# The first phase of a Fourier mixing and squared-ReLU kernel: four mirrored joins moved to the second block, small tables put on GpSimd's queue, another order

## The chip, the cores and the metric

The kernel runs on one NeuronCore of one Trainium2 chip. The metric is the device time of one execution in microseconds (us), as the median of several runs. A core has TensorE (PE in the profile; matrix products into PSUM), VectorE (DVE), ScalarE (ACT), GpSimd (POOL) and SyncE (SP, which issues most DMAs here). Each engine works through its own instructions in the order in which the program lists them and waits on semaphores for the others.

## The reference

All data are float32, with 8 sequences of 3008 rows and 256 columns.

```python
X = np.fft.fft(x, axis=1)            # x: (8, 3008, 256)
X = np.fft.fft(X, axis=2)
y = X.real.reshape(8 * 3008, 256)
h = y @ w_in                         # (256, 2048)
r = np.maximum(h, 0.0)
out = (r * r) @ w_out                # (2048, 256)
```

The real part of the double transform is a cosine transform along both axes less a sine transform along both axes.

## The kernel before, in words

**Folds.** The symmetry of sines and cosines is used before any product. Each sequence comes as seven tiles of rows (`TILES`, classes 0 to 3: one tile of class 0, one of class 1, two of class 2, three odd ones). `fold(0, t)` has six pieces. `for_p(t)` does three: a sum (line L485), the sum of mirrored columns (L501) and two combinations (L515), with a small ScalarE copy (L518) for the middle column E. `for_q(t)` does the other three: a difference (L489), L505 and two more L515. The results lie in tiles `w`, of which there are eight buffers.

**Transforms along the rows.** The products (L632) of the `w` tiles with tables of cosines and sines, `cosT` and `sinT`, collect in PSUM, for P (cosine) and Q (sine), each for even and odd columns (`kp` 0 and 1). The middle column E rides along as the last row of Q. A short radix chain joins them on VectorE: `join_4` and `join_2` put the even classes together, then `join_1` combines this with the odd part, its lower half into columns 0 to 752 of `Pt` or `Qt` (`lo`: L674 for P, L669 for Q), its mirrored upper half into columns 753 to 1504 (`hi`: L678 and L671). P's joins read PSUM and SBUF; so do Q's, which also apply signs.

**Weights.** The transform along the 256 columns is folded into `w_in`: `begin_win(j)` splits the raw 64-bit numbers of one of eight pairs of column blocks (L274, L276), ScalarE makes powers of two (L280, L281), `rounded(j)` puts halves and product together (L291, L293, L300), and TensorE multiplies with the column tables `cosd` and `sind` (L315); ScalarE copies the results to `G1` and `G2` (L316). With `shared`, a conversion on ScalarE (L283) and a product on GpSimd (L298) stand in for L300. `gE` (L324, L326) is the factor for E.

**Steps.** Then 384 steps follow: 8 sequences, 6 blocks of 251 columns each, 8 pairs `j`. `front` makes four products (L838, L839) into PSUM tiles of tag `h` (two buffers), and VectorE adds E's share and forms the sum and the difference (L841, L843, L844). `combine` squares on ScalarE (L853, L854), and from the second block on GpSimd makes four sums (L861 to L864). `back`, two steps later, multiplies with `w_out` (L878, L891). In steps 0 to 7 the remaining weights are converted; in steps 8 to 11 VectorE forms sums of `w_out` (L341 to L345). From step 10 the next sequence's folds and joins are woven into the steps.

**E.** Each front reads row E spread over all partitions (`Et`). `spread_e` makes its first 251 columns by a product (L816) and a copy (L817); `spread_rest` stores the row to DRAM and loads the other 1254 columns, both on GpSimd's queue (L821, L822).

**Order.** The scheduler is off (`manual_schedule`): the first phase is written out by hand, and each engine's and each queue's order is that of the code. Before step 0 SP issues, in this order, x tiles 0 and 1, raw win 0, x 2 and 3, `cosd`, `sind` and its last column `alt_d`, the table parts of classes 0 and 1 (six issues), x 4 and 5, those of class 2 (four), x 6, the wide tables of the odd class, raw win 1, ten small issues of `sinT`, raw win 2. `awake(n)` gives TensorE n products that fill time and that nobody reads. In steps 8 on, SP is busy with `load_column` (L408), single columns of the next sequences, and the outputs.

Of the kernel before, what the change touches and what calls it, by code (L numbers as in the profile page):

```python
# [13 lines left out]
P = 128  # L14
# [68 lines left out]
def kernel(  # L83
# [108 lines left out]
    G2 = const.tile([P, F], F32, name="G2")  # L192
    gE = const.tile([P, NFC], F32, name="gE")

    def load_table(tab, src, tiles):

        for t in tiles:
            c, r0, step, rows = TILES[t]
            for i, (s0, count) in enumerate(row_tiles(S)):
                mine = [r for r in range(count) if (s0 + r - r0) % step == 0 and 0 <= (s0 + r - r0) // step < rows]  # L200
                if mine:
                    o, m = (s0 + mine[0] - r0) // step, len(mine)
                    while m % 15 and m % 16 and o + m < P and mine[0] + step * m < P:
                        m += 1
                    nk = NC[0][c]
                    nc.sync.dma_start(out=tab[o:o + m, :, PLACE[t]:PLACE[t] + nk],
                                     in_=src[mine[0]:mine[0] + step * (m - 1) + 1:step, :, i, 0:nk])

    make_identity(nc, ident)
    last = ident[:, P - 1:]  # L210
# [394 lines left out]
    def dft_ops(b):  # L605
# [7 lines left out]
        def group(kp, which):  # L613
# [6 lines left out]
            def product(ps, c, lone_e=False, only=None):  # L620

                ts = [t for t in range(NT) if TILES[t][0] == c]
                for t in ts if only is None else ts[only:only + 1]:
                    rows = TILES[t][3]
                    if b is None:
                        w = we[0:rows, SPOT[t], kp]
                    elif lone_e:
                        w = lone[0:rows, 2 * t + kp]
                    else:
                        w = folded[b, t][0:rows, kp, PART[which]]  # L630
                        w = w if which else w[:, 0:n]
# [16 lines left out]
            def copy_4():  # L648
                a = st["a"] = hp.tile([P, 2 * P], F32, name="da", tag="da", bufs=2)[0:n]
                nc.scalar.copy(a[:, 0:n2], st["ps"][0:n, 0:n2])  # L650

            def even_part(c, lone_e):

                if c == 0 and lone_e == both_in:
                    pool, tag = (psm, ("mC", "mD")[kp]) if both_in else (psd, "d")
                    st["ps"] = pool.tile([P, 512], F32, name="pd", tag=tag)
                at, nk = EVEN[c][1:]
                product(st["ps"][:, at:at + nk], c, lone_e)
                if c == 2 and not lone_e:
                    copy_4()  # L660

            def both(lo, hi, a, ps, only=None):

                nk, nh = a.shape[-1], hi.shape[-1]
                if both_in:

                    join = nc.vector.scalar_tensor_tensor
                    if only != 1:
                        join(out=lo, in0=ps, scalar=signs[:, 0:1], in1=a, op0=ALU.mult, op1=ALU.add)  # L669
                    if only != 0:  # L670
                        join(out=hi[:, ::-1], in0=a[:, 0:nh], scalar=signs[:, 1:2], in1=ps[:, 0:nh],  # L671
                             op0=ALU.mult, op1=ALU.add)
                    return
                tt(out=lo, in0=a, in1=ps, op=ALU.add)  # L674
                if which == 1:
                    tt(out=hi[:, ::-1], in0=ps[:, 0:nh], in1=a[:, 0:nh], op=ALU.subtract)
                else:
                    tt(out=hi[:, ::-1], in0=a[:, 0:nh], in1=ps[:, 0:nh], op=ALU.subtract)  # L678

            def join_4():  # L680
                a, ps = st["a"], st["ps"]
# [2 lines left out]

            def join_2():
                a, ps = st["b"], st["ps"]
                st["c"] = hp.tile([P, NC[0][3]], F32, name="dc2", tag="dc2", bufs=2)[0:n, 0:n0]
                both(st["c"][:, 0:n1], st["c"][:, n1:n0], a, st["half"] if b != 0 else ps[:, 2 * n2:2 * n2 + n1])

            def odd_part(i, lone_e):  # L690
# [93 lines left out]
                     st["odd"], only)  # L784

            if b == 0:
                named = [("join_4", join_4), ("join_2", join_2), ("lo", join_lo), ("hi", join_hi),
                         ("join_1", join_1)]
                for i in range(3):
                    for nm, f in (("even", even_part), ("odd", odd_part)):  # L790
                        named += [(nm + ("", "_e")[e] + str(i), lambda i=i, e=e, f=f: f(i, e == 1)) for e in range(2)]
                return [((which, kp, nm), f) for nm, f in named]
            ops = [(0.0, even_n), (0.5, join_4), (0.7, join_2), (0.0, odd_n), (1.1, join_1)]
            from_psum.update((join_4, join_2, join_turned))
# [21 lines left out]
        nc.tensor.matmul(ps, last.to_broadcast([P, P]), qt[:, 0:CK], start=True, stop=True)  # L816
        nc.scalar.copy(et[:, 0:CK], ps)  # L817

    def spread_rest():
        _, qt, et = PQE[0]  # L820
        nc.gpsimd.dma_start(out=e_dram[0:1], in_=qt[P - 1:P])  # L821
        nc.gpsimd.dma_start(out=et[:, CK:], in_=e_dram[0:1, CK:].to_broadcast([P, NKT - CK]))  # L822

    def load_e(b):
        nc.sync.dma_start(out=PQE[b][2], in_=e_dram[b:b + 1].to_broadcast([P, NKT]))
# [205 lines left out]
        product()  # L1031


    start()
    awake(48)
    for t in range(2):
        load_x(0, t)
    for_p(0)
    for_q(0)
    for_p(1)  # L1040
    begin_win(0)
    load_x(0, 2)
    load_x(0, 3)
    for dst, src in ((cosd, cos_d), (sind[:, :, 0:P - 1], sin_d), (sind[:, :, P - 1:], alt_d)):
        nc.sync.dma_start(out=dst, in_=src.rearrange("(c p) m -> p c m", p=P))
    load_table(cosT, cos_s, (0, 1))
    load_x(0, 4)
    load_x(0, 5)
    load_table(cosT, cos_s, (2, 3))
    load_x(0, 6)  # L1050
    load_table(cosT, cos_s, range(ODD0, NT))
    load_table(sinT, sin_s, range(ODD0, NT))
    win[1] = load(pair_in(1))
    load_table(sinT, sin_s, range(ODD0))
    win[2] = load(pair_in(2))
    for_p(2)
    rounded(0)
    win[0][1]()
    awake(2)
    for_p(3)  # L1060
    p_part("even0", "even1")
    q_part("even_e0", "even_e1")
    awake(6)
    p_part("even2")
    q_part("even_e2")
    for_q(1)
    for_p(4)
    for_p(5)
    for_q(2)
    for_p(6)  # L1070
    p_part("odd0", "odd1", "odd2")
    q_part("odd_e0", "odd_e1", "odd_e2")
    groups[0, 0, "join_4"]()
    groups[0, 0, "join_2"]()
    for_q(4)
    groups[0, 1, "join_4"]()
    groups[0, 1, "join_2"]()
    for_q(5)
    p_part("join_1")
    for_q(6)  # L1080
    q_part("odd0", "odd1", "odd2")
    copy_e = win[0][2]()
    begin_win(1)
    for_q(3)
    q_part("even0", "even1", "even2")
    awake(12)
    rounded(1)
    for kp in range(2):
        for nm in ("join_4", "join_2", "lo"):
            groups[1, kp, nm]()  # L1090
        if kp == 0:
            begin_win(2)
    spread_e()
    q_part("hi")
    copy_e()
    spread_rest()
# [78 lines left out]
    for i in range(len(steps) + LAG + 4):  # L1175
        if i < len(steps):
            b, k0, n, j = steps[i]
            if i == NJ:
                for k in range(NX):
                    load_later(k)  # L1180
            if NJ <= i < NJ + NL:
                load_column(i - NJ)
            if i % per == 0:
                assert not side
                side = ahead(b + 1) if b + 1 < B else []
                spent, pace = 0.0, sum(t for t, _ in side) / sum(share(i + k) for k in range(per - 2))
            multiply()
            g = front(b, k0, n, j, between)
            if i < NJ:
                weights()  # L1190
                s = combine(n, g, True)
            elif i < 2 * NJ:
                if j < 4:
                    sum_wout(slice(j // 2 * (NJ // 2), (j // 2 + 1) * (NJ // 2)), j % 2)
        while finished and finished[0][0] <= i:
            store(*finished.pop(0)[1:])
        if i >= LAG and flight:
            at, g_, s_ = flight.pop(0)
# [75 lines left out]
```

## Time and profile before

| | |
|---|---|
| median of 4 runs | 1922.74 us (1919.18 to 1923.81) |
| the profiled execution | 1919.18 us, its span 1917.4 us |
| busy: PE, PEld (weight loads) | 1907.4 us (99%), 1699.2 us (89%) |
| busy: DVE, ACT, POOL | 1444.9 us (75%), 953.3 us (50%), 1120.9 us (58%) |
| DMA | 69.58 MB; 225, 240 and 260 GB/s in the first three stretches of 10 us |
| first product of step 0 | at 40.85 us |

The span runs from the first to the last instruction; the time of the execution has 1.8 us more around it. A busy share is an average over the whole span. Times in the text are from the span's start. A line of a timeline gives start, duration, engine, line, operation, written and read tiles with their sizes, and, in brackets, an idle time before it with what ended it. In the slices of the page a digit is the busy share in tenths.

### The profile page before, as it was taken

To read this page: it belongs to the slowest core of one execution; us is meant where nothing else is said; L and a number is where in the kernel's file an instruction comes from. 1 tells how busy PE (TensorE), PEld (TensorE's weight loads), DVE (VectorE), ACT (ScalarE), POOL (GpSimd) and SP (SyncE) were. 2 spreads that over 40 slices of the span, in tenths; PEclk is the share of its full clock that TensorE was granted. 3 is DMA by queue.
4 is the path that set the end of the run, shared out by engine and by line. 5 is a ranking of instruction groups with operands and counts; after the bars stand their busy time and mean duration, and the time that the engine had idled before them with its cause. 6 is when DMAs were issued, how large, how long until landed. Compare 5 with 4: busy or idle time off the path is not lost.

```text
span 1917.4 us, 28162 instructions
## 1 busy us (share of the span) xinstructions
PE 1907.4 (99%) x9270; PEld 1699.2 (89%) x9270; DVE 1444.9 (75%) x3646; ACT 953.3 (50%) x1201; POOL 1120.9 (58%) x1709
## 2 busy tenths in 40 slices
PE   9999999999999999999999999999999999999998
PEld 8888898888988898888988889888898888988887
DVE  8988887787678876788768877788767777655554
ACT  2755554555454544455544454455544555444444
POOL 0265655665566665665566665566655665566565
PEclk9999999999999999999999999999999999999999
DMA  7331201110011101111011100111001101000100
GB/s 227 116 38 28 56 28 36 28 45 13 28 36 42 34 12 36 32 43 28 12 36 47 36 20 12 47 39 34 22 20 44 36 12 22 28 12 12 22 11 23
DMA packets 146622, 69.58 MB, mean 36 GB/s; under 512 B 130145, under 2 KB 137259, under 8 KB 146474
## 3 DMA queue, kind: packets, MB, share of 16 engines
q1 hardware_dynamic: 146022, 66.87, 13.8%
q8 instruction: 73, 1.20, 0.3%
q14 instruction: 75, 0.61, 0.1%
q0 software_dynamic: 176, 0.65, 0.1%
q10 hardware_dynamic: 276, 0.26, 0.0%
HBM read 43.03 MB, written 24.69 MB: 35 GB/s over the span
## 4 chain that ended last, share of the span: by engine, by line
PE 95%; DVE 3%; DMA 0%; ACT 0%; issue 0%; POOL 0%; DVEq 0%; ACTq 0%
PE ph L838 17%; PE ph L839 17%; PE mC L891 16%; PE mA L891 16%; PE mB L891 16%; PE mD L891 8%; PE pd L740 1%; PE mA L878 1%; PE mB L878 1%; PE pd L714 1%; PE pd L632 1%; DVE w L515 0%; DMA xt<-in_x_dram 0%; PE pg L315 0%; DVE fs L485 0%
## 5 line engine op out<-in xcount | busy, mean ns | idle before, releaser
L853 ACT ACTIVATE g<-g 128x1004 f32<-128x1004 f32 (+1 forms) x384 | 399.3, 1040 | 691.4 <-DVE g L844 445.9
L841 DVE SCALAR_TENSOR_TENSOR he<-Et,gE,ph 128x251 f32<-128x251 f32 (+1 forms) x768 | 362.5, 472 | 342.9 <-PE ph L839 338.5
L861 POOL TENSOR_TENSOR s<-g 128x251 f32<-128x251 f32 (+1 forms) x376 | 236.6, 629 | 636.8 <-ACT g L854 576.4
L838 PE MATMUL ph<-Pt,G 128*128 128x251 f32 (+1 forms) x1536 | 452.5, 375 | 0.4 <-DVE g L844 0.3
L839 PE MATMUL ph<-Qt,G 127*128 127x251 f32 (+1 forms) x1536 | 451.3, 374 | 0.0
L854 ACT ACTIVATE g<-g 128x1004 f32<-128x1004 f32 (+1 forms) x384 | 399.6, 1041 | 12.2
L891 PE MATMUL mC<-s,wsum 128*128 128x251 f32 (+1 forms) x1504 | 381.4, 374 | 0.0
L891 PE MATMUL mA<-g,wout 128*128 128x251 f32 (+1 forms) x1504 | 380.1, 374 | 0.0
L843 DVE TENSOR_TENSOR g<-he,ph 128x251 f32<-128x251 f32 (+1 forms) x768 | 320.4, 417 | 53.5 <-POOL s L861 1.4
L839 PEld LDWEIGHTS ph<-Qt,G 127*128 127x128 f32 x1536 | 291.3, 190 | 35.7
L838 PEld LDWEIGHTS ph<-Pt,G 128*128 128x128 f32 x1536 | 285.5, 189 | 34.6 <-DVE g L844 0.8
L891 PEld LDWEIGHTS mC<-s,wsum 128*128 128x128 f32 x1504 | 285.5, 190 | 34.5
L844 DVE TENSOR_TENSOR g<-he,ph 128x251 f32<-128x251 f32 (+1 forms) x768 | 314.0, 409 | 0.0
L891 PEld LDWEIGHTS mA<-g,wout 128*128 128x128 f32 x1504 | 282.6, 189 | 35.2 <-issue 0.3
L862 POOL TENSOR_TENSOR s<-s,g 128x251 f32<-128x251 f32 (+1 forms) x376 | 270.6, 720 | 29.5
L863 POOL TENSOR_TENSOR s<-g 128x251 f32<-128x251 f32 (+1 forms) x376 | 272.3, 724 | 0.0
L864 POOL TENSOR_TENSOR s<-g,s 128x251 f32<-128x251 f32 (+1 forms) x376 | 241.7, 643 | 0.0
L891 PE MATMUL mB<-g,wsum 128*128 128x251 f32 (+1 forms) x752 | 220.4, 374 | 0.0
L891 PE MATMUL mD<-s,wout 128*128 128x251 f32 (+1 forms) x752 | 220.3, 374 | 0.0
L891 PE MATMUL mB<-s,wout 128*128 128x251 f32 (+1 forms) x752 | 219.9, 374 | 0.0
L891 PEld LDWEIGHTS mB<-g,wsum 128*128 128x128 f32 x752 | 142.6, 190 | 17.4
L891 PEld LDWEIGHTS mD<-s,wout 128*128 128x128 f32 x752 | 141.9, 189 | 17.7
(176 smaller groups left out, 1386.1 us busy)
## 6 DMA issues: line engine op xcount, KB each, us to landing
out_dram<-os SPq DMA_DIRECT2D x376, 56.0 KB
xt<-in_x_dram SPq DMA_DIRECT2D x39, 384.0 KB
xt<-in_x_dram SPq DMA_DIRECT2D x63, 128.0 KB
Et<-e_dram SPq DMA_DIRECT2D x7, 752.5 KB
out_dram<-os SPq DMA_DIRECT2D x288, 6.8 KB
raw<-in_moe_w_in_dram SPq DMA_DIRECT2D x16, 256.0 KB
raw<-in_moe_w_out_dram SPq DMA_DIRECT2D x16, 256.0 KB
xt<-in_x_dram SPq DMA_DIRECT2D x2, 512.0 KB
```

The costliest lines, as they stand in the source:

```text
L838: nc.tensor.matmul(hP, G1[:, fs], pt[:, ks], start=True, stop=True)
L839: nc.tensor.matmul(hQ, G2[0:P - 1, fs], qt[0:P - 1, ks], start=True, stop=True)
L841: nc.vector.scalar_tensor_tensor(out=t, in0=et[:, ks], scalar=gE[:, fc:fc + 1], in1=hP, op0=ALU.mult, op1=ALU.add)
L843: tt(out=g[:, h, 0, 0:n], in0=t, in1=hQ, op=ALU.add)
L844: tt(out=g[:, h, 1, 0:n][:, ::-1], in0=t, in1=hQ, op=ALU.subtract)
L853: act(v, v, AF.Relu)
L854: act(v, v, AF.Square)
L861: gt(out=s1, in0=g21, in1=g22, op=ALU.add)
L862: gt(out=s2, in0=s1, in1=g11, op=ALU.subtract)
L863: gt(out=s3, in0=g11, in1=g21, op=ALU.subtract)
L864: gt(out=s4, in0=g12, in1=s2, op=ALU.subtract)
L891: nc.tensor.matmul(acc[nm][:, i, 0:n], w, v[:, 0:n], start=j == 0 and i == 0, stop=j == NJ - 1, skip_group_check=True)
```

## The change

1. The mirrored halves (`hi`) of the first sequence's last joins, P's and Q's, are no longer made before step 0, but in steps 8 to 11, one in each. Until then the odd parts are copied from PSUM to `w` buffers by ScalarE (`keep`), and Q's joined even part is put in a `w` buffer too.
2. E's spread is cut at column 753: the lower part as before on GpSimd's queue, the upper part stored by SP in step 9 and loaded in step 11.
3. The table parts of classes 0 to 2 of `cosT` and `sinT` (20 issues) and `alt_d` go to GpSimd's queue; SP issues the rest.
4. The order of folds, products and joins is another one; win 1's product goes to GpSimd (`shared`), and win 2's split stands behind Q's lower joins.
5. A ScalarE copy of one element stands at the start, ahead of the first fold's copy. The filling products are 48 + 10 instead of 48 + 2 + 6 + 12.

```diff
-    def load_table(tab, src, tiles):
+    def load_table(tab, src, tiles, queue=nc.sync):
...
+            def held_w():
+                return wp.tile([P, 2, D], F32, name="w", tag="w").rearrange("p a d -> p (a d)")[0:n, 0:n0]
+
+            def keep():
+                o = held_w()
+                nc.scalar.copy(o, st["odd"])
+                st["odd"] = o
...
-    def spread_rest():
+    KH = S // 4 + 1
+
+    def spread_lower():
         _, qt, et = PQE[0]
-        nc.gpsimd.dma_start(out=e_dram[0:1], in_=qt[P - 1:P])
-        nc.gpsimd.dma_start(out=et[:, CK:], in_=e_dram[0:1, CK:].to_broadcast([P, NKT - CK]))
+        nc.gpsimd.dma_start(out=e_dram[0:1, 0:KH], in_=qt[P - 1:P, 0:KH])
+        nc.gpsimd.dma_start(out=et[:, CK:KH], in_=e_dram[0:1, CK:KH].to_broadcast([P, KH - CK]))
+
+    def store_upper():
+        nc.sync.dma_start(out=e_dram[0:1, KH:], in_=PQE[0][1][P - 1:P, KH:])
+
+    def load_upper():
+        nc.sync.dma_start(out=PQE[0][2][:, KH:], in_=e_dram[0:1, KH:].to_broadcast([P, NKT - KH]))
...
     start()
     awake(48)
+    load_x(0, 0)
+    load_x(0, 1)
+    nc.scalar.copy(turn[0:1, 0, 0:1], ident[0:1, 0:1])
+    load_table(cosT, cos_s, (0, 1), nc.gpsimd)
+    folds_of("P0 Q0 P1 Q1")
     begin_win(0)
     load_x(0, 2)
     load_x(0, 3)
...
+    load_table(cosT, cos_s, (TWO, TWO + 1), nc.gpsimd)
+    for t in range(ODD0, NT):
+        load_x(0, t)
     load_table(cosT, cos_s, range(ODD0, NT))
+    load_table(sinT, sin_s, range(ODD0), nc.gpsimd)
     load_table(sinT, sin_s, range(ODD0, NT))
     win[1] = load(pair_in(1))
     win[2] = load(pair_in(2))
+    folds_of("P2")
     rounded(0)
+    products_of("P0 P1")
     win[0][1]()
+    products_of("E0 E1")
+    folds_of("P3")
+    products_of("P2 P3")
+    p_part("copy")
+    products_of("E2 E3")
+    folds_of("P4 P5 Q2 P6 Q3 Q4")
+    products_of("P4 P5 P6 E4 E5 E6 Q0 Q1 Q2 Q3")
+    for nm in ("join_4", "join_2", "lo"):
+        groups[0, 0, nm]()
+    folds_of("Q5")
+    for nm in ("join_4", "join_2", "lo"):
+        groups[0, 1, nm]()
+    p_part("keep")
+    q_part("copy")
+    products_of("Q4 Q5")
     copy_e = win[0][2]()
+    begin_win(1, True)
+    folds_of("Q6")
+    products_of("Q6")
+    awake(10)
+    for nm in ("join_4", "join_2"):
+        groups[1, 0, nm]()
+    halves, product, _ = win[1][0]
+    halves()
+    product()
+    for nm in ("join_4", "join_2"):
+        groups[1, 1, nm]()
+    q_part("lo")
+    copy_e()
     spread_e()
+    begin_win(2)
+    q_part("keep")
+    spread_lower()
...
                     sum_wout(slice(j // 2 * (NJ // 2), (j // 2 + 1) * (NJ // 2)), j % 2)
+                    groups[j < 2, j % 2, "hi"]()
+                    if j % 2:
+                        (store_upper if j == 1 else load_upper)()
```

`folds_of` calls `for_p` and `for_q`, `products_of` the products of one tile for both `kp` (P, Q, or E for the middle column).

More of the change, by code (lines that the diff above doesn't have):

```diff
@@ L205, in load_table @@
                     nk = NC[0][c]
-                    nc.sync.dma_start(out=tab[o:o + m, :, PLACE[t]:PLACE[t] + nk],
-                                     in_=src[mine[0]:mine[0] + step * (m - 1) + 1:step, :, i, 0:nk])
+                    queue.dma_start(out=tab[o:o + m, :, PLACE[t]:PLACE[t] + nk],
+                                    in_=src[mine[0]:mine[0] + step * (m - 1) + 1:step, :, i, 0:nk])
     make_identity(nc, ident)
@@ L650, in copy_4, with even_part @@
                 nc.scalar.copy(a[:, 0:n2], st["ps"][0:n, 0:n2])
-            def even_part(c, lone_e):
+            def even_part(c, lone_e, only=None):
                 if c == 0 and lone_e == both_in:
@@ L657, in even_part @@
                 at, nk = EVEN[c][1:]
-                product(st["ps"][:, at:at + nk], c, lone_e)
-                if c == 2 and not lone_e:
-                    copy_4()
+                product(st["ps"][:, at:at + nk], c, lone_e, only)
             def both(lo, hi, a, ps, only=None):
@@ L673, in both @@
                     return
-                tt(out=lo, in0=a, in1=ps, op=ALU.add)
+                if only != 1:
+                    tt(out=lo, in0=a, in1=ps, op=ALU.add)
+                if only == 0:
+                    return
                 if which == 1:
@@ L686, in join_2 @@
                 a, ps = st["b"], st["ps"]
-                st["c"] = hp.tile([P, NC[0][3]], F32, name="dc2", tag="dc2", bufs=2)[0:n, 0:n0]
+                st["c"] = held_w() if both_in else hp.tile([P, NC[0][3]], F32, name="dc2", tag="dc2", bufs=2)[0:n, 0:n0]
                 both(st["c"][:, 0:n1], st["c"][:, n1:n0], a, st["half"] if b != 0 else ps[:, 2 * n2:2 * n2 + n1])
@@ L786, in group @@
             if b == 0:
[L787 to L791, printed above, removed]
+                named = [("copy", copy_4), ("join_4", join_4), ("join_2", join_2), ("lo", join_lo), ("keep", keep),
+                         ("hi", join_hi)]
+                for e in range(2):
+                    for t in range(NT):
+                        c = TILES[t][0]
+                        f = odd_part if c == 3 else even_part
+                        args = (t - ODD0, e == 1) if c == 3 else (c, e == 1, t - TWO if c == 2 else None)
+                        named.append((("", "e")[e] + str(t), lambda f=f, args=args: f(*args)))
                 return [((which, kp, nm), f) for nm, f in named]
@@ L1031, in rounded, with folds_of, products_of @@
         product()
+    def folds_of(names):
+        for nm in names.split():
+            (for_p if nm[0] == "P" else for_q)(int(nm[1:]))
+    def products_of(names):
+        for nm in names.split():
+            (p_part if nm[0] == "P" else q_part)({"P": "", "Q": "", "E": "e"}[nm[0]] + nm[1:])
     start()
     awake(48)
[L1036 to L1040, printed above, removed]
+    load_x(0, 0)
[3 more added lines that the diff above has]
+    folds_of("P0 Q0 P1 Q1")
     begin_win(0)
@@ L1043 @@
     load_x(0, 3)
[L1044 to L1050, printed above, removed]
+    for dst, src, queue in ((cosd, cos_d, nc.sync), (sind[:, :, 0:P - 1], sin_d, nc.sync), (sind[:, :, P - 1:], alt_d, nc.gpsimd)):
+        queue.dma_start(out=dst, in_=src.rearrange("(c p) m -> p c m", p=P))
@@ L1051 @@
+    load_table(cosT, cos_s, (TWO, TWO + 1), nc.gpsimd)
+    for t in range(ODD0, NT):
+        load_x(0, t)
     load_table(cosT, cos_s, range(ODD0, NT))
+    load_table(sinT, sin_s, range(ODD0), nc.gpsimd)
     load_table(sinT, sin_s, range(ODD0, NT))
     win[1] = load(pair_in(1))
-    load_table(sinT, sin_s, range(ODD0))
     win[2] = load(pair_in(2))
-    for_p(2)
+    folds_of("P2")
     rounded(0)
+    products_of("P0 P1")
     win[0][1]()
-    awake(2)
-    for_p(3)
-    p_part("even0", "even1")
@@ L1062 @@
[L1062 to L1081, printed above, removed]
-    copy_e = win[0][2]()
-    begin_win(1)
@@ L1084 @@
[L1084 to L1092, printed above, removed]
+    products_of("E0 E1")
[7 more added lines that the diff above has]
+        groups[0, 0, nm]()
@@ L1093 @@
+    folds_of("Q5")
[4 more added lines that the diff above has]
+    products_of("Q4 Q5")
+    copy_e = win[0][2]()
+    begin_win(1, True)
[11 more added lines that the diff above has]
+    copy_e()
     spread_e()
-    q_part("hi")
@@ L1095 @@
-    copy_e()
-    spread_rest()
+    begin_win(2)
+    q_part("keep")
+    spread_lower()
     LAG = 2
```

## The prediction

> **What bounds the kernel now.** I read four views: the page, to find which engine sets the pace; the chain of waits on TensorE, to find where it doesn't; the busy time by stretch; and VectorE's timeline over the first 60 us. The page first:
>
> ```profile
> span 1917.4 us, 28162 instructions
> ...
> PE   9999999999999999999999999999999999999998
> ...
> DVE  8988887787678876788768877788767777655554
> ...
> PEclk9999999999999999999999999999999999999999
> ```
>
> After the first slices TensorE (PE) is full at the full granted clock, so the diff, which removes no product from the steps, can only gain before TensorE is full. TensorE's waits between 38 and 60 us, longest first (waiting line, releaser, us in total, times, longest):
>
> ```profile
> PE pe L816 <- DVE Qt L669: 1.5, 1, 1.5
> PE pe L324 <- ACT G L316: 0.9, 2, 0.5
> PE mA L878 <- POOL wout L298: 0.6, 1, 0.6
> PE ph L838 <- DVE g L844: 0.3, 1, 0.3
> ```
>
> Busy time by stretch, columns PE, PEld, DVE, ACT, POOL, clock, DMA share, GB/s:
>
> ```profile
> 4.40:40.30 35.90, 34.39 (x220) 29.39 (x219) 34.45 (x91) 8.45 (x20) 0.00 (x0) 1.00 0.87 240
> 40.30:58.90 18.60, 16.66 (x78) 13.44 (x78) 17.45 (x42) 13.38 (x22) 4.05 (x4) 1.00 0.38 140
> 58.90:95.00 36.10, 36.10 (x180) 32.27 (x180) 32.94 (x77) 28.14 (x42) 7.56 (x5) 1.00 0.38 125
> ```
>
> VectorE (DVE) is busy 34.45 of 35.90 us in the first stretch (the rest are gaps of some hundredths between dependent instructions), 17.45 of 18.60 in the second; only from 58.9 is TensorE without a pause (36.10 of 36.10). TensorE's 34.39 in the first stretch is partly the filling products of `awake`, which nobody waits for. So the first phase is a queue of VectorE work from the landing of x's first tile (4.43) to the last lower join of Q (issued 39.66), and what leaves this queue ends the kernel earlier by its own length. VectorE's timeline where the change cuts:
>
> ```profile
> 28.67 0.54 DVE L678 TENSOR_TENSOR Pt<-dc,pd 128x376 f32<-128x376 f32 x1
> ...
> 29.58 0.54 DVE L678 TENSOR_TENSOR Pt<-dc,pd 128x376 f32<-128x376 f32 x1
> ...
> 35.19 0.69 DVE L300 SCALAR_TENSOR_TENSOR win<-m,fd 128x512 f32<-128x512 f32 x1
> ...
> 37.66 0.42 DVE L274 TENSOR_SCALAR fd<-raw 128x512 uint32<-128x512 uint32 x1
> 37.99 0.42 DVE L276 TENSOR_SCALAR m<-raw 128x512 uint32<-128x512 uint32 x1
> ...
> 39.66 0.61 DVE L669 SCALAR_TENSOR_TENSOR Qt<-pd,signs,dc 128x376 f32<-128x376 f32 x1
> 40.18 1.11 DVE L671 SCALAR_TENSOR_TENSOR Qt<-dc,signs,pd 128x376 f32<-128x376 f32 x2
> 41.21 0.15 DVE L326 TENSOR_SCALAR gE<-pe 128x2 f32<-128x2 f32 x1
> 41.95 0.48 DVE L841 SCALAR_TENSOR_TENSOR he<-Et,gE,ph 128x251 f32<-128x251 f32 x1 [0.59 <-PE ph L839]
> ```
>
> **Part by part, VectorE.** I count from one start to the next, since neighbours overlap by some 0.08 us.
> - P's two mirrored joins leave: 28.67 to 29.12 and 29.58 to 30.03, 0.45 each: 0.90 us, on the path.
> - `begin_win(1, True)` gives the product L300 to GpSimd (POOL): 35.19 to 35.79, 0.60, on the path. In its place come a 0.61 us ScalarE conversion (L283's row) and a POOL product of 1.27 to 1.51 (L298's rows). L293 now waits for L283; by the sum below VectorE splits win 1 at 30.70 and reaches L293 at 34.9, while ScalarE needs 0.72 + 0.72 + 0.61 after the split: done by 34.1 even if the copy of P's second odd part holds it until 32. The POOL product is done by 37.0; its readers, the L315 products behind step 0, come at 40.4. Cost 0.
> - `begin_win(2)`'s split (37.66 to 38.32, 0.66) moves behind Q's lower joins. There VectorE has nothing but gE (0.15) until L841: 39.66 + 0.61 to 41.95 is 1.68 us of TensorE and ScalarE (L816, L838, L839, copy of Et). 0.26 + 0.66 fit: 0.66 gained.
> - Q's mirrored joins (40.18 to 41.21) also leave, but lay in that 1.68 us: gain 0. Without them VectorE idles there more.
> - Folds only change places: Q1's 1.58 us now precedes win 0's split, so P2 and P3 start 1.58 later (11.62, 15.14); P4, P5, Q2, P6 start at 16.73, 18.33, 19.93 and 21.51, as they did.
>
> Sum: 0.90 + 0.60 + 0.66 = 2.16 us. The last lower join ends near 38.1 instead of 40.27, and steps 0 to 2, whose VectorE work is the same, follow.
>
> **The mirrored joins in the second block.** Four joins come into steps 8 to 11 (95 to 114 us): 0.45 to 0.52 from their old rows; with both inputs in SBUF and GpSimd at work up to 0.4 more, as the sums there show (L342: 0.69 at 98.25, 1.09 at 107.59). VectorE idles 0.46, 0.87 and 0.50 after the sums of steps 8, 9 and 10, and not after step 11. So I expect at most 0.9 us of lateness at step 12's L841 (114.11). Who waits: TensorE's first product of step 13 (117.50) reuses the PSUM tile that the first L844 of step 12 frees at 115.38, 2.1 us ahead. Cost 0; if that cover were gone, 0.9. The new copies of the odd parts (four, PSUM to SBUF, 377 wide) lie between the 251-wide L817 (0.37) and the 502-wide L901 (0.58): some 0.47 each on ScalarE, 8.45 busy of 35.90. Q's two stand before the copies of G (43.61 before, 41.45 now); with win 2's two powers ScalarE is free at about 41.7, so the first copy is 0.3 late, the second, whose result L324 waits for, not. Cost 0 to 0.3; I take 0.
>
> **SP.** It sheds 21 small issues (20 of table parts, one of alt_d), 20.0 us of its queue: 5.55 + 0.47 + 2.71 + 11.25. Behind them stood x's tiles 4 to 6, the wide tables and the raw win 1 and 2, which now go out earlier. In steps 9 and 11 it gets the store and load of E's upper part, between the columns `xe` that fill its queue (24 issues in 22.83 us from 95.67): two issues of about 0.95, so what follows is about 2 us late: outputs, and x's later tiles. The tile issued at 139.82 is folded at 192.1: covered. E's upper part is first read in block 3, some 60 us on; the load of E took 3.8 us to land. Cost 0.
>
> **Does the data still come?** DMA runs full until 28.5 us and then has nothing to do:
>
> ```profile
> 10.00:11.50 1.50, 0.69 (x1) 1.00 0.70 138
> 11.50:13.00 1.50, 0.00 (x0) 1.00 0.53 107
> ...
> 26.50:28.00 1.50, 0.68 (x1) 1.00 1.05 235
> ...
> 29.50:31.00 1.50, 0.69 (x1) 1.00 0.15 34
> ```
>
> (VectorE's busy time on x's tiles alone, then clock, DMA share, GB/s). In before some 7.1 MB (the sum of such stretches) had come by 28.5: all but the small sin tables (0.43 MB) and win 2. The holes at 10 to 13 us are SP issuing small tables; at 290 GB/s (the mean from 13 to 28) they would hold 0.50 MB more, which is where those tables now go. So raw win 1 lands at 28.5 to 29.5, and VectorE asks at 30.70 (31.62 before): margin 1.2 to 2.2 us, the thinnest here. The wide cos table is in by about 24; P's first lower join needs its products at 27.24.
>
> **GpSimd's 21 issues.** The nearest rows:
>
> ```profile
> 41.60 0.70 POOL L821 DMA_DIRECT2D e_dram<-Qt  x1 [38.46 <-DVE gE L326]
> 43.93 0.57 POOL L822 DMA_DIRECT2D Et<-e_dram  x1 [1.62 <-DMA e_dram<-Qt]
> ```
>
> POOL is free from 3.13. At 0.70 each the last small sin table is issued by 17.8 and, with the 2.0 us the store L821 took to land, there at 20; the products want it from about 28. From that landing on, TensorE still has Q's products before it, 0.9 + 1.3 + 2.5 + 0.4 + 1.3 = 6.4 us by the rows of L632 and L324, and Q's first lower join asks for them at 36.9; so a landing up to 30.4 is free, which is 1.2 us per issue. Do these issues slow VectorE? Beside L822 the pair L274 and L276 took 0.44 and 0.41 against 0.42: between 0 and 21 x 0.03 = 0.6 us in all by this row; beside POOL arithmetic, a farther row, up to 0.4 each. I take 0 and keep 0.6 for the range.
>
> The Trainium skill speaks against this move: "SBUF — State Buffer", section "SBUF: two separate sides", says that a DMA issued from GpSimd has its descriptors written by GpSimd itself and starves while VectorE runs an operation that uses both SBUF ports; a DMA of 620 ns took about 3100 so. By that, an estimate from the page is 2.5 us for the one issue that meets win 0's split, which changes no sum; for all 21 it would be 52 us. The row above shows no lengthening beside such a pair.
>
> The filling products drop from 68 to 58. By my times TensorE's longest pause is 1.1 us, ahead of L816, against 1.5 now at clock 1.00. Cost 0.
>
> **Sum.** The profiled execution took 1919.18, its span 1917.4 plus 1.8 around it; the median of the four runs is 1922.74, 3.6 above. Less 2.16: 1917.0 by the one, 1920.6 by the median; I predict 1920.5.
>
> **Rivals.** A measurement of this kernel tells about 0.2% (3.8 us) from no change; the four runs alone lie 4.6 apart.
> - *A, forecast, -2.2*: 0.55, its own range -3.4 to -0.8. Of it 0.03 falls beyond 3.8 by the scatter.
> - *B, more is gained.* TensorE's waits in steps 0 to 2 (0.9 + 0.6 + 0.3, with roundings 1.9) shrink too, because GpSimd and ScalarE come earlier to them: -4.1, 1918.6. For: the win products and ScalarE's conversions are reordered just ahead of them. Against: VectorE is 17.45 of 18.60 busy there, with unchanged work. 0.27.
> - *C, slower: GpSimd's issue rate.* The tables are on one queue at an unknown pace. From 1.2 us per issue on, each further 0.1 delays Q's joins by 2.1; at 1.6 the loss is 8.4 - 2.2 = +6.2, 1928.9. It turns into a loss at 1.3 and passes 0.2% at 1.49. For: 64 to 256 pieces in each, where L821 moved 7 and L822 128. Against: 0.57 for 128 pieces. 0.15, 0.01 of it within 0.2%.
> - *D, it does nothing:* raw win 1 lands 2.2 us after VectorE asks, and the gain is waited away: 0. 0.03, of which 0.01 beyond.
>
> Faster: 0.03 + 0.27 = 0.30; slower: 0.14 + 0.01 = 0.15; within: 0.55. The range leaves out most of C and the edge of B: 1917.2 to 1924.5.
>
> **What would show it.** Right: in the changed profile VectorE without a wait over 0.3 us from 4.4 to 38; the last lower join of Q issued near 37.5; the first L838-type product of step 0 near 38.7; full TensorE from 56.8; idle VectorE after the sums of steps 8 to 10 gone and TensorE still full there. Wrong: VectorE waiting for a raw win, TensorE waiting for a small table, POOL's DMA rows over 1.2 us, folds longer than 0.68, or a TensorE pause near 100 to 120 us.

## The result and the profile after

The changed kernel took 1918.56 us in the median of 41 runs (1917.44 to 1923.13), the kernel before 1921.61 in the median of 61 (1919.18 to 1923.86). The ratio is 0.9986, 95% interval 0.9982 to 0.9991: 2.7 us less by the ratio, between 1.7 and 3.5, and 3.05 by the two medians. That is inside 0.2%, as was forecast, with -2.2.

A single profile misleads here. The profiled execution of before (1919.18) was the fastest of its 61, that of the changed kernel (1921.01) one of the slowest of its own: by spans, 1917.4 and 1919.2, the change would have lost 1.8 us. Lines have moved: L838, L839, L841, L816 and L878 are L858, L859, L861, L828 and L898 now, P's joins L673 (lower) and L679, Q's L667 and L669. Both kernels were profiled again, as before_again (1920.34, span 1918.5) and after_again (1918.88, span 1917.1). before_again's profile is of the fastest of its eleven executions, after_again's of the slowest, so these two lie closer together than the medians. A product in float32 is two records of the profile: the 48 products of `awake(48)` stand there as x96.

The first profile after, busy time by stretch (PE, PEld, DVE, ACT, POOL, clock, DMA share, GB/s), up to where the prediction had the first phase end, and in one stretch of 2 us:

```profile
4.40:38.10 33.70, 32.48 (x172) 27.18 (x172) 29.30 (x78) 7.08 (x20) 10.90 (x19) 0.90 1.06 279
22.00:24.00 2.00, 2.00 (x8) 2.00 (x8) 1.90 (x6) 0.65 (x4) 0.50 (x1) 0.50 1.09 207
```

VectorE is no longer a queue without gaps: 29.30 of 33.70. And TensorE's clock, 1.00 in all of the first 160 us before, was granted at 0.50 here. TensorE's timeline shows the pause ahead of it and the price, then VectorE's timeline who paid:

```profile
20.61 1.60 PE L632 MATMUL pd<-cosT,w 92*128 92x189 f32 x4 [0.95 <-DVE fd L489]
24.51 5.40 PE L632 MATMUL pd<-cosT,w 128*128 128x377 f32 x12
```

```profile
29.32 0.55 DVE L673 TENSOR_TENSOR Pt<-dc,pd 128x377 f32<-128x377 f32 x1 [2.15 <-PE pd L632]
```

The twelve records of the second line take 3.96 us at clock 1.00 (the next group, at 29.75). VectorE waited 2.15 us for those that P's first lower join reads. In after_again the clock was 1.00, and the wait is another one:

```profile
33.07 0.43 DVE L274 TENSOR_SCALAR fd<-raw 128x512 uint32<-128x512 uint32 x1 [1.58 <-DMA raw<-in_moe_w_in_dram]
38.97 1.12 DVE L667 SCALAR_TENSOR_TENSOR Qt<-pd,signs,w 128x377 f32<-128x377 f32 x2
41.78 0.48 DVE L861 SCALAR_TENSOR_TENSOR he<-Et,gE,ph 128x251 f32<-128x251 f32 x1 [0.95 <-ACT Et L829]
```

VectorE stands 1.58 us before the split of win 1, because the raw weight has not landed; Q's two lower joins start at 38.97. Behind the first phase nothing changed. TensorE's waits from 38 to 60 us of the first profile after, and its busy time in after_again from the stretch where it was full before:

```profile
PE pe L324 <- ACT G L316: 0.9, 2, 0.5
PE mA L898 <- POOL wout L298: 0.6, 1, 0.6
PE ph L858 <- DVE g L864: 0.3, 1, 0.3
```

```profile
58.90:95.00 36.10, 36.10 (x179) 32.25 (x179) 32.90 (x77) 28.33 (x42) 7.57 (x5) 1.00 0.40 125
```

The three waits of steps 0 to 2 are those of before, to the tenth; the 1.5 us ahead of the spread is not there (0.75 in after_again). From 60 to 150 us all kernels but the run hi_back show TensorE full alike (35.00 of 35.00, 55.00 of 55.00). So a kernel's time here is read off the start of its first L858-type product: 40.85 in before, 42.05 in before_again, 42.62 and 40.67 in the two of after, spans in the same order; from there to the end of the span all four take 1876.4 to 1876.6 us.

### The profile page after: what moved, and what is told of

It is laid out like the page before. It is cut to its first block, busy times and chain, and to the rows that moved or that the text cites. A ratio compares the mean times of both kernels' runs of the same rounds, so it can differ in the third digit from the quotient of the medians.

```text
span 1919.2 us, 28146 instructions
## 1 busy us (share of the span) xinstructions
PE 1909.5 (99%) x9250; PEld 1700.4 (89%) x9250; DVE 1444.0 (75%) x3645; ACT 955.6 (50%) x1207; POOL 1134.4 (59%) x1731
## 4 chain that ended last, share of the span: by engine, by line
PE 96%; DVE 2%; DMA 0%; ACT 0%; issue 0%; SPq 0%; POOL 0%; DVEq 0%; ACTq 0%
PE ph L858 17%; PE ph L859 17%; PE mC L911 16%; PE mA L911 16%; PE mB L911 16%; PE mD L911 8%; PE pd L632 2%; PE pd L749 1%; PE mA L898 1%; PE mB L898 1%; PE pd L723 1%; PE pg L315 0%; DVE w L515 0%; DVE he L861 0%; DVE fs L485 0%
## 5 line engine op out<-in xcount | busy, mean ns | idle before, releaser
L861 DVE SCALAR_TENSOR_TENSOR he<-Et,gE,ph 128x251 f32<-128x251 f32 (+1 forms) x768 | 362.4, 472 | 343.7 <-PE ph L859 337.6
L858 PE MATMUL ph<-Pt,G 128*128 128x251 f32 (+1 forms) x1536 | 452.5, 375 | 0.4 <-DVE g L864 0.3
L859 PE MATMUL ph<-Qt,G 127*128 127x251 f32 (+1 forms) x1536 | 451.3, 374 | 0.0
L859 PEld LDWEIGHTS ph<-Qt,G 127*128 127x128 f32 x1536 | 291.3, 190 | 35.7
L858 PEld LDWEIGHTS ph<-Pt,G 128*128 128x128 f32 x1536 | 285.5, 189 | 34.5 <-DVE g L864 0.8
L911 PEld LDWEIGHTS mA<-g,wout 128*128 128x128 f32 x1504 | 282.6, 189 | 35.3 <-issue 0.3
L882 POOL TENSOR_TENSOR s<-s,g 128x251 f32<-128x251 f32 (+1 forms) x376 | 270.8, 720 | 29.5
```

The costliest lines, as they stand in the source:

```text
L858: nc.tensor.matmul(hP, G1[:, fs], pt[:, ks], start=True, stop=True)
L859: nc.tensor.matmul(hQ, G2[0:P - 1, fs], qt[0:P - 1, ks], start=True, stop=True)
L861: nc.vector.scalar_tensor_tensor(out=t, in0=et[:, ks], scalar=gE[:, fc:fc + 1], in1=hP, op0=ALU.mult, op1=ALU.add)
L882: gt(out=s2, in0=s1, in1=g11, op=ALU.subtract)
L911: nc.tensor.matmul(acc[nm][:, i, 0:n], w, v[:, 0:n], start=j == 0 and i == 0, stop=j == NJ - 1, skip_group_check=True)
```

## The experiments

Each ran beside the kernel before on the same chip; "before" is the median there. The ratio, with its 95% interval, is an estimate of its own and not the quotient of the two medians; the two differ by up to 0.0005, which is 0.9 us.

| run | median | before | ratio |
|---|---|---|---|
| before_again | 1921.27 | 1920.92 | 1.0001 (0.9992 to 1.0010) |
| after_again | 1918.30 | 1920.92 | 0.9984 (0.9975 to 0.9993) |
| fill_8 | 1918.38 | 1920.92 | 0.9986 (0.9977 to 0.9995) |
| tab2_on_sp | 1918.92 | 1920.92 | 0.9991 (0.9982 to 1.0000) |
| tables_only | 1921.11 | 1921.33 | 0.9997 (0.9988 to 1.0005) |
| hi_only | 1922.12 | 1921.33 | 1.0001 (0.9992 to 1.0010) |
| win1_late | 1919.78 | 1921.33 | 0.9994 (0.9985 to 1.0003) |
| hi_back | 1926.33 | 1921.33 | 1.0026 (1.0017 to 1.0035) |
| hi_back_pool | 1919.34 | 1921.69 | 0.9992 (0.9983 to 1.0000) |
| win1_first | 1918.51 | 1921.69 | 0.9988 (0.9979 to 0.9997) |
| fills_moved | 1918.85 | 1920.95 | 0.9988 (0.9979 to 0.9997) |
| fills_and_win1 | 1917.62 | 1920.95 | 0.9982 (0.9974 to 0.9991) |

Executions of one kernel scatter by 1.5 to 6 us, so neighbours in this table are often not told apart by time, and the timelines decide.

**The two kernels again.**

before_again: no edit.

> The kernel before, unchanged, for a second profile. Its first profile is of the fastest of its executions (1919.2 where the median is 1921.6). Theory 1 (VectorE's queue sets the first phase, and TensorE's granted clock adds scatter): the ratio is 1.000 within 0.0005, the time some 1921.5, and the typical execution differs from the first profile only before 60 us, by waits of VectorE for x's tiles or for products, 1.5 to 3 us in all, with the clock at 1.00. Rival (the scatter belongs to the steps, far behind the first phase): the first product of step 0 starts at 40.9 again and the 2 us are found after 100 us.

after_again: no edit.

> The changed kernel, unchanged, for a second profile: its first one is of a slow execution (1921.0 where the median is 1918.6), with the granted clock at half from 20.6 to 27.3 us. Theory 1: ratio 0.9986; a typical execution has the clock at 1.00, no wait of 2 us for P's lower join, and the first product of step 0 at 38.7 to 39.5 instead of 42.6. Rival (the small tables on GpSimd's queue land late in every execution, and that alone holds P's products): VectorE waits for P's products by about 2 us again, whatever the clock, and step 0 starts after 41.

before_again shows waits that the first profile of before lacks. One line of TensorE's timeline, then one of VectorE's:

```profile
24.23 2.88 PE L632 MATMUL pd<-cosT,w 128*128 128x377 f32 x8 [0.75 <-DMA cosT<-in_cos_s_dram]
```

```profile
36.99 0.32 DVE L669 SCALAR_TENSOR_TENSOR db<-pd,signs,da 128x95 f32<-128x95 f32 x1 [0.92 <-ACT da L650]
```

A part of the wide cosine table is late, TensorE's later products move back, and VectorE waits 0.92 us for the copy of Q's sums. So before, too, was held by a table load in such an execution; the prediction's base had none of this.

**More filling products early.**

```diff
-    products_of("P2 P3")
+    products_of("P2")
+    awake(8)
+    products_of("P3")
```

> The changed kernel with eight filling products more, between the products of P2 and those of P3, where TensorE paused 0.95 us and the granted clock then fell to a half. Theory 1 (the pause lets the clock fall, and the half clock makes P's products late): clock 1.00 from 4 to 40 us, no wait of VectorE for P's first lower join, median 1917.6 to 1918.2, and hardly an execution above 1919.5. Rival (the late tables themselves hold P's products, the clock is a side show): VectorE still waits about 2 us for P's products and the median stays at 1918.6, with a tail to 1922.

In its profile the clock is 1.00 and P's lower joins wait for nobody, but the time is the changed kernel's. VectorE waits 1.20 us for the raw weight at 32.70. And TensorE, now later by the fills, runs its last ten filling products from 38.01 to 40.24, starts the spread only then, and VectorE waits 1.31 us for `Et`. The half clock does not set the typical time: after_again had none either. It may be behind the longest ones: four of the changed kernel's 41, 1921.01 to 1923.13 us, have a mean granted clock of 0.998, which no shorter one has. fill_8 doesn't test this, for after_again beside it had no such execution.

**One table back on SP's queue.**

```diff
-    load_table(cosT, cos_s, (TWO, TWO + 1), nc.gpsimd)
+    load_table(cosT, cos_s, (TWO, TWO + 1))
```

> The changed kernel with the four parts of the cosine table of class 2 issued by SP again, ahead of x's tiles 4 to 6; the other small parts stay on GpSimd's queue. In the profile of the changed kernel those on GpSimd's queue land 6.4 to 8.3 us after their issue, the last at about 20.7, which is when P3's products start. If lateness of these four matters, P3's products start near 18.5, TensorE does not pause ahead of them, the clock stays at 1.00, and the median is 1917.6 to 1918.2. If GpSimd's queue is harmless, nothing changes, or x's tile 4 comes late to its fold (16.6) because SP issues it 2.7 us later: 1918.6 to 1920.

TensorE waited 2.62 us for the wide cosine table behind these issues, and after it the clock was 0.50 from 24 to 26 us. VectorE waited 1.35 us for a tile of x, which the expectation had as a risk. By time the run is not told apart from the changed kernel.

**Parts of the change alone.** tables_only is the kernel before with its 20 small table parts and `alt_d` on GpSimd's queue, in the old order:

```diff
-    load_table(cosT, cos_s, (0, 1))
+    load_table(cosT, cos_s, (0, 1), nc.gpsimd)
...
```

> The kernel before with only the tables moved: the 20 small parts and alt_d on GpSimd's queue, all else as before. In the second profile of the kernel before TensorE waits 0.7 us for the second part of the wide cosine table, and VectorE then 0.9 us for a copy of Q's products. Theory 2: SP reaches the wide tables some 8 us earlier, these two waits go, and the time falls by 0.9 to 1.5: 1919.7 to 1920.3. Theory 1: SP's queue is off the path: 1921.2. Against both: the small parts land 6 to 8 us after issue on GpSimd's queue, and the last sine parts (needed at about 34) or win 1 come late: 1921.5 to 1923.

No difference: -0.2 us by the medians. In its profile TensorE didn't wait for the wide cosine table, and VectorE waited 0.28 for Q's copy instead of 0.92.

hi_only keeps the old order and queues and moves only the four upper joins to steps 8 to 11, with `keep`, `spread_lower` and SP's store and load:

```diff
-    q_part("hi")
     copy_e()
-    spread_rest()
+    q_part("keep")
+    spread_lower()
```

> The kernel before with only the mirrored joins moved to steps 8 to 11 (with the copies, the cut spread of E and its two DMAs on SP); tables, win 1 on VectorE and the order as before. Theory 1: 0.90 us less, 1920.4. Theory 2: VectorE waits for a copy of Q's products in a typical execution of the kernel before (0.9 us in its second profile), so the 0.90 turns into a longer wait: 1921.0 to 1921.3, step 0 starts no earlier than 41.8.

Nothing gained. VectorE's timeline shows what took the joins' place:

```profile
32.66 0.43 DVE L274 TENSOR_SCALAR fd<-raw 128x512 uint32<-128x512 uint32 x1 [1.07 <-DMA raw<-in_moe_w_in_dram]
44.85 0.48 DVE L861 SCALAR_TENSOR_TENSOR he<-Et,gE,ph 128x251 f32<-128x251 f32 x1 [1.62 <-PE ph L859]
```

P's two joins, 0.9 us, became a wait of 1.07 for the raw weight (before_again asked for it at 31.80 and had it), and Q's two became part of a 1.62 us wait in the spread, which was 0.59 with them. The prediction had the second, not the first. This execution also waited 1.15 us for Q's copy (before_again 0.92) and 0.56 for tiles of x, so the profile shows that the joins' time was not gained, not that the raw weight alone took it.

**The split of win 1 later.** Win 1's split behind Q6's fold, its halves and product behind the spread, and two filling products instead of ten:

```diff
-    begin_win(1, True)
     folds_of("Q6")
     products_of("Q6")
-    awake(10)
+    begin_win(1, True)
+    awake(2)
...
     spread_e()
+    halves()
+    product()
```

> The changed kernel with win 1's split moved behind Q6's folds, its two halves (1.32 us) behind Q's lower joins, and 2 filling products instead of 10 ahead of the spread. Theory 2: the wait of 1.2 to 1.6 us for raw win 1 goes, 1.3 of work moves into the time in which VectorE waits for the spread; then TensorE's chain (Q6's products end at 37.0) and Q's joins set the end: the first product of step 0 at 38.3 to 39.0 instead of 40.7, less 0.6 by which the splits now overrun the spread: 1916.6 to 1917.3, the fastest so far. Theory 1 (no waits that matter, the queue alone): 0.7 us less than the changed kernel, 1917.7.

The raw weight was there when VectorE asked (33.06), but VectorE then waited 1.09 us for Q's products, which stood behind 1.35 us of TensorE's waits for the wide cosine table, and GpSimd's product met win 2's split: L276 took 1.52 us instead of 0.42. The wait moved, and the median is no better than the changed kernel's.

**The upper joins back.** All four joins at their places in the first phase, with the upper store and load on SP right after `spread_lower`:

```diff
-    p_part("keep")
+    p_part("hi")
...
-    q_part("keep")
+    q_part("hi")
     spread_lower()
+    store_upper()
+    load_upper()
```

> The changed kernel with the mirrored joins back in the first phase, at the places which they had: P's behind the lower joins, Q's behind the spread; everything else as changed. Theory 1 (VectorE's queue sets the first phase, as the prediction has it): P's two joins cost their 0.90 us again, Q's nothing: 1919.3 where the changed kernel has 1918.4, and step 0 starts 0.9 later. Theory 2 (landings bound both kernels: in a typical execution of the changed one VectorE waits 1.2 to 1.6 us for raw win 1): the joins lie ahead of that wait and shrink it by 0.9; step 0 starts as before, within 0.3 us, and the time is 1918.4.

It lost 5.0 us to before. SP's queue shows why, and VectorE's timeline what follows:

```profile
16.06 7.46 SPq L259 DMA_DIRECT2D raw<-in_moe_w_in_dram  x4
41.04 0.26 SPq L839 DMA_DIRECT2D e_dram<-Qt  x1
42.69 1.22 SPq L259 DMA_DIRECT2D raw<-in_moe_w_in_dram  x2
```

```profile
49.09 0.43 DVE L274 TENSOR_SCALAR fd<-raw 128x512 uint32<-128x512 uint32 x1 [5.74 <-DMA raw<-in_moe_w_in_dram]
```

The store waits for Q's upper join, and eight loads of raw weights wait behind it on the in-order queue; in the first profile after the last of them is issued by 35.3 us. VectorE stands 5.74 us. TensorE stands 5.63 us behind it, and then the granted clock was 0.50 (stretch of 2 us, columns as above; the eight records behind the pause take 3.96 us, against 2.06 at clock 1.00):

```profile
52.00:54.00 2.00, 2.00 (x5) 1.64 (x6) 1.89 (x6) 1.51 (x2) 0.04 (x1) 0.50 0.07 28
```

The joins themselves were not at fault: VectorE had no pause from 20 us to the end of step 0, and L861 came at 40.93, earlier than in after_again. So the next run gave the whole row to GpSimd's queue:

```diff
-        nc.gpsimd.dma_start(out=e_dram[0:1, 0:KH], in_=qt[P - 1:P, 0:KH])
+        nc.gpsimd.dma_start(out=e_dram[0:1], in_=qt[P - 1:P])
...
-    store_upper()
-    load_upper()
```

> The changed kernel with all four upper joins back in the first phase at their places (P's after its lower joins, Q's after the first columns are spread), and the whole row sent to memory and back by GpSimd's queue, as before the change; nothing of it is left in the steps, and no store or load of it stands in SP's queue. The run hi_back showed VectorE without a pause from 20 us to the end of step 0 (L861 first at 40.93, 0.85 earlier than in after_again, although four joins more were in front of it), and then 5.74 us of waiting for a raw weight whose load stood in SP's queue behind the store of Qt (issued at 41.04). Theory 1 (the joins were free in the first phase; hi_back's whole loss is SP's queue): L861 of step 0 at 40.9 to 41.8, no wait for the raw weight of step 2, time as the changed kernel's: 1918.0 to 1918.9 where before gives 1921.3. Theory 2 (P's two joins are on the path, as the prediction's 0.90 has it): 0.9 us over the changed kernel, 1919.3. Theory 3 (all four were on the path): 2.0 over it, 1920.4.

Of the 7.8 us that hi_back stood over the changed kernel, 7.0 are back: they were SP's queue, with the half clock behind it. What is left, 0.8 by the medians (0.3 to 0.7 by the distances to before on the same chip, 1.2 to 1.5 by the ratios), is nearest to the second theory, though the intervals overlap. VectorE's timeline has the joins in the place of after_again's wait:

```profile
31.07 0.99 DVE L679 TENSOR_TENSOR Pt<-dc,pd 128x376 f32<-128x376 f32 x2
31.98 0.42 DVE L274 TENSOR_SCALAR fd<-raw 128x512 uint32<-128x512 uint32 x1
```

The reading is that P's joins are on the path where the raw weight is in time, and free where it is late. The profiles compared under "The sum" below show the first half; the second is argued from hi_only.

**The raw weight first.**

```diff
-    load_table(sinT, sin_s, range(ODD0, NT))
     win[1] = load(pair_in(1))
+    load_table(sinT, sin_s, range(ODD0, NT))
```

> The changed kernel with one line moved: the load of the second raw weight is issued ahead of the wide parts of the sine table instead of behind them. In after_again VectorE waited 1.58 us for that weight (landed about 33.1) and TensorE waited 0.7 for the last join of Q after it. Theory 1 (the raw weight's landing is on the path): the wait for it is gone, L861 of step 0 comes 0.7 to 1.2 us earlier (TensorE's chain is the next limit), time 0.7 to 1.2 under the changed kernel: 1917.1 to 1917.6 where before gives 1921.3. Theory 2 (the memory queue is full until 36 us, so the order only chooses who is late): the wide sine table lands 1.8 us later (512 KB at 285 GB/s), TensorE's products Q4 to Q6 wait for it, VectorE waits for their copies, and the time is the changed kernel's or up to 1 us over it: 1918.3 to 1919.3.

The wait for the raw weight is gone (L274 at 31.51), the time is not. TensorE's timeline, then VectorE's:

```profile
38.48 2.39 PE L228 MATMUL filled<-ident 128*128 128x128 f32 x20
40.72 0.59 PE L828 MATMUL pe<-Qt,ident 128*128 128x251 f32 x2
```

```profile
42.25 0.47 DVE L861 SCALAR_TENSOR_TENSOR he<-Et,gE,ph 128x251 f32<-128x251 f32 x1 [1.83 <-ACT Et L829]
```

TensorE, late by 1.06 us of waiting for the wide cosine table and 1.25 of waiting for VectorE, starts its ten filling products when VectorE starts Q's last lower joins (38.56), and the spread L828 stands behind all of them. The time is in the second theory's range, but for another reason: the fills, not the sine table, became the wait.

**The fills moved.** Eight of the last ten filling products are put between the products of P2 and P3 (fills_moved); with the raw weight first as well (fills_and_win1):

```diff
-    products_of("P2 P3")
+    products_of("P2")
+    awake(8)
+    products_of("P3")
...
-    awake(10)
+    awake(2)
```

> The changed kernel with eight of its last ten filling pairs (20 products, 2.39 us in one group of TensorE's timeline) put between the products of P2 and P3, as in fill_8, and two pairs left ahead of the spread of Q's last row. In fill_8 the fills ended at 40.24 and the spread's product L828 started there, with VectorE then waiting 1.31 us for the spread; in win1_first they ran from 38.48 and L828 followed without a pause. Theory 1 (the last fills are on TensorE's path whenever it is late): L828 starts when the last lower join of Q is done, VectorE's wait for the spread is 0.3 to 1.0 (the spread's own length after the join), and the time is 0.3 to 1.0 under fill_8's and the changed kernel's: 1917.5 to 1918.2 where before gives 1921.5. Theory 2 (the fills fill a pause only, and VectorE's raw weight sets the time): the time is the changed kernel's, 1918.4 to 1918.6. Theory 3 (two pairs are too few to hold the clock through steps 0 to 2): some of the executions show a clock of 0.998 and take 1921 and more, and the median is above 1919.

> As fills_moved, with the load of the second raw weight ahead of the wide sine table too, as in win1_first, where VectorE didn't wait for it but TensorE's ten filling pairs and its late products set the time. Theory 1 (raw weight and last fills each bound in turn, so only both together show): 0.7 to 1.5 under the changed kernel, 1917.1 to 1917.9. Theory 2 (TensorE's wait for the wide cosine table at 22 to 24 us, 0.6 to 1.1, sets the time whatever is moved behind it): 1918.2 to 1918.6. Theory 3 (clock, as in fills_moved): above 1919.

By its median fills_moved alone is no faster than the changed kernel. The 2.1 us under before on its chip fit only the third theory's times (over 1919 where before gives 1921.5), but no execution shows the clock of 0.998 that this theory names. And its profiled execution (1917.70) shows the first theory's picture: L828 waits 1.00 us for Q's join, not the reverse. What held the others, up to 1920.29, was not seen. Both together gave 1917.62, in the first theory's range by the medians; by the distances to before on the same chip it is 0.3 to 0.7 us under the changed kernel, the theory's lower edge at best. All 11 executions lie between 1917.09 and 1918.56. Two lines of TensorE's timeline, two of VectorE's:

```profile
37.43 0.61 PE L228 MATMUL filled<-ident 128*128 128x128 f32 x4
38.68 0.69 PE L828 MATMUL pe<-Qt,ident 128*128 128x251 f32 x2 [0.64 <-DVE Qt L667]
```

```profile
31.39 0.42 DVE L274 TENSOR_SCALAR fd<-raw 128x512 uint32<-128x512 uint32 x1
37.50 1.12 DVE L667 SCALAR_TENSOR_TENSOR Qt<-pd,signs,w 128x377 f32<-128x377 f32 x2
```

Ahead of Q's lower joins VectorE waits for nobody, and they start at 37.50, 1.47 earlier than in after_again. This is the lowest median of the study: 0.9 us under the changed kernel, 3.3 under before on its chip; its interval (0.9974 to 0.9991) overlaps the changed kernel's, so that it is faster is not shown.

## Why the prediction was right, point by point

**The first phase is VectorE's queue.** Half right. It held for the execution that the prediction read, the best of before. In before_again and in both profiles of the changed kernel VectorE waited 0.9 to 2.2 us in one place, for late data or for TensorE's products behind late data or a half clock. The prediction itself named VectorE waiting for a raw weight as a sign of being wrong, and after_again shows that wait. The base was off too: the median of four runs, 1922.74, stands 1.1 above that of 61, which is more than half of the distance between 1920.5 and 1918.56.

**The sum, 0.90 + 0.60 + 0.66 = 2.16.** Three profiles let it be read without late data: in the first of before, in hi_back_pool and in fills_and_win1 VectorE shows no wait from its first fold to Q's lower joins. The first fold of each, in this order, then the first L861 of the last two (before's L841, at 41.95, stands in the prediction):

```profile
4.46 0.69 DVE L485 TENSOR_TENSOR fs<-xt 95x512 f32<-95x512 f32 x1 [2.88 <-DMA xt<-in_x_dram]
4.38 0.69 DVE L485 TENSOR_TENSOR fs<-xt 95x512 f32<-95x512 f32 x1 [2.81 <-DMA xt<-in_x_dram]
4.70 0.69 DVE L485 TENSOR_TENSOR fs<-xt 95x512 f32<-95x512 f32 x1 [3.12 <-DMA xt<-in_x_dram]
40.67 0.48 DVE L861 SCALAR_TENSOR_TENSOR he<-Et,gE,ph 128x251 f32<-128x251 f32 x1
40.31 0.48 DVE L861 SCALAR_TENSOR_TENSOR he<-Et,gE,ph 128x251 f32<-128x251 f32 x1 [0.95 <-ACT Et L829]
```

From fold to step 0 that is 37.49, 36.29 and 35.61 us. So the order with GpSimd's product and win 2's split is worth 1.20 (1.26 was counted), and P's joins 0.68 more (0.90 counted; 0.91 where win 1 is split, at 31.98 and 31.39). Q's joins cost 0: hi_back_pool has them, and its L861 follows them without a wait. In all 1.88 of the 2.16. These are single executions, and the parts of the 1.20 were not run one by one; ScalarE's early copy and the fewer filling products are in it too. By time the parts are less certain: from tables_only to hi_back_pool the distance to before goes from -0.2 to -2.4, 2.1 by the medians and 1.0 by the ratios.

The total measured, 1.7 to 3.5, holds both 1.88 and 2.16, but in part by luck. After the change a typical execution waits for the raw weight, which the sum left out, and before it a typical one waits too (0.92 us in before_again), so that the two work against each other; how much of the 2.7 comes from either was not separated. (In the third bullet gE's 0.26 should be the 0.15 of its row; both fit.)

**The joins in steps 8 to 11 cost 0.** Right. VectorE's timeline after, the two of P:

```profile
110.37 1.06 DVE L679 TENSOR_TENSOR Pt<-dc,w 128x376 f32<-128x376 f32 x1
115.49 0.54 DVE L679 TENSOR_TENSOR Pt<-dc,w 128x376 f32<-128x376 f32 x1
```

The four take 0.60, 0.60, 1.06 and 0.54 (the long one behind a sum of 1.10, both beside GpSimd), and TensorE is 25.00 of 25.00 us busy from 93 to 118. SP's two issues took 2.07 and 1.51 us in after_again, where some 0.95 was counted, and delayed nobody there. The `keep` copies behind the spread showed no cost: L324's wait is 0.9 in all, as before.

**Does the data still come?** This is the term that was mis-sized: not "28.5 to 29.5" but 33.07 in after_again, 32.70 in fill_8 and 31.91 in fills_moved. The old holes did fill. From 10 to 13 us before moved 122 GB/s, and after_again this (columns as above):

```profile
10.00:13.00 3.00, 3.00 (x30) 3.00 (x29) 2.90 (x8) 1.26 (x3) 2.42 (x5) 1.00 1.11 267
```

But the rest was slower: 262 instead of 275 from 4.4 to 10 us, and 271 at a DMA share of 1.07 from 13 to 28, where before moved 288 at 1.02 and the prediction took 290. Up to 28.5 us both had moved the same, 250 and 249 GB/s, so the 0.43 MB of small sine tables were in only because as much else was not. Two more things were not told apart: SP now issues the raw weights of win 2 and 3 in one go with win 1's (six issues from 17.13; before, two at 20.34 and four at 32.93), and hi_only, with the old queues and order, had its weight at 32.66 as well. The margin that the prediction called the thinnest was negative: 0.2 to 1.6 us of the gain were waited away in these three, rival D's mechanism at a part of its price. With the load issued ahead of the wide sine table (win1_first, fills_and_win1) the wait is gone.

**GpSimd's 21 issues.** The price of an issue was right, that of a landing was not. GpSimd's timeline in after_again, and one kind in its view of transfers (KB each, median us from issue to landing):

```profile
12.47 2.14 POOL L206 DMA_DIRECT2D sinT<-in_sin_s_dram  x4
```

```profile
sinT<-in_sin_s_dram POOLq DMA_DIRECT2D x5, 23.8 KB, 6.8
```

An issue took 0.54 (2.14 / 4) to 0.74, and with the waits between them the 21 took 17.3 us, 0.82 each, so rival C, from 1.2 on, is out. The landing took 6.4 to 8.0 us, not 2.0. The Trainium skill, page "DMA: Bandwidth & Descriptors", section "Anatomy of one DMA — SWDGE (gpsimd) path", gives about 2.0 us plus bytes over 436 GB/s, from which an estimate for 23.8 KB is 2.1. The measured 6.8 beside a full memory queue decides here. The last part, issued by 21.1, was in by about 28 (no landing of `sinT` took over 7.6), two us ahead of its products (30.59), so the point held. The rule of starving descriptors that the prediction weighed ("SBUF — State Buffer", section "SBUF: two separate sides") doesn't show in the time of the issues: the three around win 0's split, 10.58 to 12.48 us, took 0.63 each. Whether it is in the landing was not told apart from the full queue.

**The filling products cost 0.** Wrong, and so is "which nobody waits for" in the first paragraph. A fill stands in TensorE's order like any product. The last ten, 2.39 us, stood ahead of the spread whenever TensorE was late (fill_8, win1_first). Fewer early ones left a thin stretch, behind which the clock fell in the first profile after; that they would have prevented it is argued, since after_again kept its clock without them.

**Rival B.** Out: the waits of steps 0 to 2 are unchanged at 0.9, 0.6 and 0.3. The median lies near its 1918.6, but from other terms.

**What would show it.** The lower joins of Q were to be issued near 37.5 and step 0's first product near 38.7. The changed kernel starts its two lower joins at 38.97 and the product at 40.67; fills_and_win1, without the two waits, at 37.50 and 39.20.

## What to carry to other kernels

Before pricing work that leaves a queue, list who is next: the data, with their landing times from several executions, and the other engines' in-order work. Here taking some 2 us out of VectorE's queue exposed a load and a group of filling products; the version that mends both has the lowest median. A store that waits for a late result doesn't belong on the queue that feeds the next loads, and filling products belong where TensorE is idle and nothing late stands behind them.

## What the runs showed of the hardware

- In the first profile after, TensorE's clock fell to 0.50 behind a thin stretch: from 16 to 22 us TensorE was busy 4.78 of 6.00 us, its longest wait 0.95. The Trainium skill, page "TensorE: Matmul & The Clock Gate", section "What's actually happening", has the half clock after an idle window of about 3.4 us. Here it fell sooner: by the clock of the stretches (0.93 in 48 to 49 and in 22 to 24 us) an estimate is 2.6 us into hi_back's pause of 5.63 and 2.3 into tab2_on_sp's of 2.62, and in this profile no pause came near either. Yet in win1_first TensorE was busy 5.69 of 8.00 us from 20 to 28 at clock 1.00, and before waited 1.53 ahead of the spread at 1.00, so neither a thin stretch nor such a pause decides it alone. What does stays open.
- Memory transfers from GpSimd's queue landed 6.4 to 8.0 us after issue beside a full memory queue.
- VectorE's L276, 0.42 us alone, took 1.52 beside GpSimd's product L298 (1.39 us), once, in win1_late.
